# Windowed attention with sinks feeding a maxout FFN: another order for the opening and for chunk 3

## The chip, the cores and the metric

The kernel runs on one core of one Trainium2 chip. A core has five engines that run at the same time, each working through its own queue strictly in order: PE (TensorE, matrix products into PSUM), DVE (VectorE), ACT (ScalarE), POOL (GpSimd) and SP (SyncE, which here only issues transfers). PEld is the loading of weights into PE's array, which the profile lists apart from the products. Sixteen DMA engines, shared by all queues, move data between HBM (the main memory) and SBUF (the memory on the chip). PSUM, which takes PE's results, has 8 banks. The metric is the device time of one execution in microseconds (us), lower being better; a kernel's time is the median of its runs.

## The reference

The first half is attention over a window of 128 positions plus 4 sink positions, in 4 batches of 8 heads, 768 positions and 64 dimensions per head:

```python
scores = scale * np.matmul(q, k.transpose(0, 1, 3, 2))
keep = is_sink | in_window               # pos < 4, or 0 <= i - j < 128
scores = np.where(keep, scores, -1000000000.0)
a = np.exp(scores - max); a = a / (sum(a) + 1e-09)
attn = np.matmul(a, v)
```

The second half takes the heads side by side as `x` (3072 tokens of 512 numbers) through a feed-forward layer whose hidden part is the largest of three products:

```python
h = np.maximum(np.maximum(x @ w1, x @ w2), x @ w3)     # 3072 x 768
out = h @ w_out                                        # 3072 x 512
```

All inputs and the output are float32; the kernel computes in bfloat16 with float32 sums.

## The kernel before

The 3072 tokens are cut into 12 chunks of 256, three to a batch. `ci` is a chunk and `p` one of four pairs of heads; chunk 0 is the first of its batch and has no chunk ahead of it, so that its scores have three blocks (`lo = 1`), while chunk 1 has four and the sinks besides. The steps of a chunk are functions of the same name as here:

- `load` (L76) brings 512 KB of q, k or v in float32 into one of two buffers, on SP's queue. A `gate` is a tiny POOL instruction that writes into the buffer first, so that the transfer waits for POOL: `after(wi, c)` (L434) reads column c of weight `wi`, and so waits until the piece of the weight that holds this column has landed; `pool_gate` (L440) is a bare write.
- `cast_qk` and `cast_v` (L95, L104) turn this into bfloat16 on the engine named in the call. g = 0 stands for the pairs 0 and 1, g = 1 for the pairs 2 and 3.
- `turn` and `turn2` (L109, L129) are four PE transposes of q or k and a copy out of PSUM. From chunk 4 on `turn_dma` (L150) does this by a transposing transfer.
- `premask` (L251) lays the additive mask into the two PSUM banks of a pair of heads; `score` (L259) adds the products of q and k; `expo` (L282) takes the exponential on ACT and frees the banks. A pair without a `premask` is masked afterwards by a product on DVE, `mask` (L289).
- `sink_k`, `sink_score`, `sink_v` and `av_open` do the sinks. `av` (L339) multiplies by v, and divides on DVE (a reciprocal and a product) into `x_sb`.
- `xpose` (L364) is the turn of `x`: for each half t of the 256 tokens four PE transposes and one copy.
- `ffn_h(ci, fp, wi)` (L383) makes a third of the hidden layer for one of the three weights: 8 products over the columns 256 fp to 256 fp + 255 of weight `wi`, then a copy on ACT (`wi` = 0) or a maximum on DVE. `ffn_y` (L406) makes half of the output rows.
- `load_w` (L234) and `load_wo` bring the weights on POOL's queue. The transfer turns float32 into bfloat16, and its sizes are those of the bfloat16 side: 256 columns of a weight are 256 KB in the profile.
- `warm(n)` (L172) is n products of zeros, whose result is not used.

The order of the work is written out by hand. Each line of the list at L454-772 appends its instructions to the queues of the engines that it uses; nothing is reordered later. A queue waits at its first instruction whose inputs, or whose target (a buffer or a PSUM bank still being read), are not ready. PSUM banks are handed out in the order in which they were given back. The list is free until chunk 3; then `for i in range(3, NCH)` repeats a fixed interleaving in which chunk i's feed-forward part covers chunk i + 1's attention.

In what follows a third of a weight is named by its columns: w0[512:768] is the last third of the first of the three weights (`moe_w1` in the inputs), w1 is the second, w2 the third.

Of the kernel before, what the change touches and what calls it, by code (L numbers as in the profile page):

```python
# [9 lines left out]
F32 = mybir.dt.float32  # L10
# [6 lines left out]
def kernel(  # L17
# [13 lines left out]
    nc = tc.nc  # L31
# [3 lines left out]
    d_model = H * D  # L35
# [13 lines left out]
    with tc.manual_schedule():  # L49
# [122 lines left out]
        def warm(n):  # L172

            if n:
                pw = bank([128, 512], F32, "warm")
                for _ in range(n):
                    nc.tensor.matmul(pw, lhsT=wz[:, 0:128], rhs=wz, start=True, stop=True)  # L177
                give(pw)
# [160 lines left out]
        def av(ci, p):  # L339
            b, c = divmod(ci, CPB)  # L340
            o = os_[ci, p]
            e = es[ci, p][0]
            first = c == 0
            for t in range(2):
                for a in range(2):
                    blocks = [(1, ci, 0)] if t == 0 else [(2, ci, 0), (3, ci, 1)]
                    if t == 0 and c:
                        blocks = [(0, ci - 1, 1)] + blocks
                    for s, cv, n in blocks:
                        nc.tensor.matmul(  # L350
                            o[:, t, a], lhsT=e[:, a, s], rhs=vb[cv % RING][:, n, 2 * p + a],
                            start=first, stop=True, skip_group_check=True)
# [27 lines left out]

        hs = {}

        def ffn_h(ci, fp, wi, cuts=1):  # L383
            if ci not in hs:
                hs[ci] = work.tile([128, FB, 256], BF16, tag="h", bufs=3, name="h_sb")
            hp = bank([128, 2, 256], F32, "h_ps")
            for f in range(2):
                c0 = (2 * fp + f) * 128
                for ds in range(DS):
                    nc.tensor.matmul(  # L390
                        hp[:, f].rearrange("q (i t r) -> q i t r", i=2, t=2),
                        lhsT=w_sb[wi][:, ds, c0:c0 + 128],
                        rhs=xTs[ci][:, :, ds].rearrange("q t (i r) -> q i t r", i=2),
                        start=(ds == 0), stop=(ds == DS - 1))
            dst = hs[ci][:, 2 * fp:2 * fp + 2]
            if wi == 0:
                nc.scalar.copy(dst, hp)  # L397
            else:
                for f in range(cuts):
                    x = slice(2 * f // cuts, 2 * (f + 1) // cuts)  # L400
                    nc.vector.tensor_max(dst[:, x], dst[:, x], hp[:, x])  # L401
            give(hp)
# [2 lines left out]

        def ffn_y(ci, t, eng=None):  # L406
            if t == 0:
                ys[ci] = work.tile([128, 2, d_model], F32, tag="y", bufs=2, name="y_sb")
            yp = bank([128, d_model], F32, "y_ps")
            for fb in range(FB):  # L410
                nc.tensor.matmul(yp, lhsT=hs[ci][:, fb, t * 128:(t + 1) * 128], rhs=wo[:, fb],  # L411
                                 start=(fb == 0), stop=(fb == FB - 1))
            (nc.scalar.copy if eng is None else eng.tensor_copy)(ys[ci][:, t], yp)  # L413
            give(yp)

        def ffn_y_part(ci, t, c0, c1, eng):
            if t == 0 and c0 == 0:
                ys[ci] = work.tile([128, 2, d_model], F32, tag="y", bufs=2, name="y_sb")
# [36 lines left out]
        warm(5)  # L455
        load(0, 'k')
        load(0, 'q', part=0, parts=2)
        warm(2)
# [5 lines left out]
        warm(7)  # L464
        cast_qk(0, 'k', 0, nc.vector)
        cast_qk(0, 'k', 1, nc.gpsimd)
        cast_qk(0, 'q', 0, nc.gpsimd)
        premask(0, (0,))
        cast_qk(0, 'q', 1, nc.scalar)
        turn(0, 'k', 0, nc.vector)  # L470
        turn(0, 'k', 1, nc.scalar)
        turn(0, 'q', 1, nc.scalar)
        premask(0, (3,))
        load(1, 'k')
        turn(0, 'q', 0, nc.vector)
        score(0, (0,))
        premask(0, (2,))
        cast_v(0, 0, 0, nc.vector)
        cast_v(0, 1, 0, nc.gpsimd)
        cast_v(0, 1, 1, nc.vector)  # L480
        cast_qk(1, 'k', 0, nc.vector)
        premask(0, (1,))
        load(1, 'q')
        load_w(0, 512, 768)
        load_w(0, 0, 512)
        score(0, (1,))
        score(0, (2,))
        expo(0, 0)
        warm(3)
        sink_k(0)  # L490
        cast_v(0, 0, 1, nc.vector)
        expo(0, 1)
        load_w(1, 512, 768)
        turn2(1, 'k', 0, nc.vector)
        expo(0, 2)
        cast_qk(1, 'k', 1, nc.scalar)
        av_open(0)
        cast_qk(1, 'q', 0, nc.scalar)
        av(0, 0)
        score(0, (3,))  # L500
        sink_v(0)
        cast_qk(1, 'q', 1, nc.gpsimd)
        load_w(1, 0, 512)
        av(0, 1)
        load(1, 'v')
        expo(0, 3)
        turn(1, 'k', 1, nc.scalar)
        turn(1, 'q', 1, nc.vector)
        turn2(1, 'q', 0, nc.vector)
        cast_v(1, 0, 0, nc.gpsimd)  # L510
        cast_v(1, 1, 1, nc.gpsimd)
        cast_v(1, 1, 0, nc.gpsimd)
        cast_v(1, 0, 1, nc.gpsimd)
        premask(1, (0,))
        av(0, 3)
        load(2, 'k', part=0, parts=2, gate=after(0, 300))
        score(1, (0,))
        score(1, (2,))
        av(0, 2)
        load_w(2, 0, 256)  # L520
        load(2, 'k', part=1, parts=2)
        premask(1, (3,))
        score(1, (3,))
        expo(1, 0)
        xpose(0, 0, nc.vector)
        expo(1, 2)
        load(2, 'q', part=1, parts=2)
        load(2, 'q', part=0, parts=2, gate=pool_gate)
        xpose(0, 1, nc.vector)
        load_w(2, 256, 512)  # L530
        sink_score(1)
        load_w(2, 512, 768)
        premask(1, (1,))
        score(1, (1,))
        av_open(1)
        cast_qk(2, 'k', 1, nc.gpsimd)
        mask(1, 2)
        expo(1, 3)
        load(2, 'v', gate=after(0, 300))
        expo(1, 1)  # L540
        av(1, 0)
        load(3, 'q', gate=after(2))
        ffn_h(0, 2, 0)
        av(1, 2)
        av(1, 3)
        av(1, 1)
        cast_qk(2, 'k', 0, nc.scalar)
        load(3, 'k')
        ffn_h(0, 0, 0)
        ffn_h(0, 2, 1)  # L550
        ffn_h(0, 1, 0)
        xpose(1, 0, nc.vector)
        xpose(1, 1, nc.vector)
        ffn_h(0, 1, 1)
        ffn_h(1, 0, 0)
        ffn_h(0, 0, 1)
        load_wo()
        factors(msk0, addm0)
        ffn_h(1, 2, 0)
        turn(2, 'k', 0, nc.vector)  # L560
        ffn_h(1, 1, 0)
        ffn_h(1, 1, 1)
        turn(2, 'k', 1, nc.scalar)
        cast_v(2, 1, 0, nc.gpsimd)
# [64 lines left out]
        cast_v(3, 0, 0, nc.gpsimd)  # L629
# [12 lines left out]
        mask(3, 3)  # L642
# [173 lines left out]
```

## Time and profile before

| what | value |
|---|---|
| time, median of 3 runs | 178.46 us (178.2 to 179.15) |
| the profiled execution | 178.04 us, of which the span of the profile is 176.3 us |
| PE | 169.8 us busy, 96% of the span |
| PEld / DVE / ACT / POOL | 127.0 / 120.7 / 86.0 / 66.4 us busy |
| moved by DMA | 34.90 MB, 198 GB/s over the span |
| read from HBM / written | 25.17 MB / 6.29 MB |
| granted TensorE clock, mean | 0.997 |

The difference between 178.04 and 176.3 us lies ahead of the first and behind the last instruction of the profile. A busy PE is no sign that PE is at its best: the warm products count as busy, and the durations of pipelined products overlap. The distance between the starts of two products is what each of them takes of PE's time, and in the chain of work that ended last the pieces are given by that distance. The sixteen DMA engines together can show a busy share over 1, since packets overlap.

### The profile page before, as it was taken

What the parts mean: (1) busy time and instruction counts of PE and PEld (TensorE: products, weight loads), DVE (VectorE), ACT (ScalarE), POOL (GpSimd) and SP (SyncE); (2) the same over time, 40 slices, a digit from 0 to 9 for tenths busy, and PEclk for the clock granted to TensorE, in tenths of its full rate; (3) what the DMA queues carried; (4) which work ended last, traced back from release to release, by engine and by line L of the source; (5) the groups of instructions that cost most, each with busy time, mean ns of one, the idle gap of its engine ahead of it and who ended that gap; (6) DMA issues with size and microseconds to landing.
All of it is one profiled execution on the core that took longest, in us unless ns stands there. A gap on an engine that the chain in (4) does not pass through costs nothing.

```text
span 176.3 us, 4635 instructions
## 1 busy us (share of the span) xinstructions
PE 169.8 (96%) x1864; PEld 127.0 (72%) x1877; DVE 120.7 (68%) x262; ACT 86.0 (49%) x172; POOL 66.4 (38%) x126
## 2 busy tenths in 40 slices
PE   7889999999999999999999999999999999999992
PEld 2545999866786697697696796796795795796871
DVE  3387644796697895775775874875785775976451
ACT  4298455758844914914715814814617616420210
POOL 7596507623494693182172054245244000000000
PEclk9999999999999999999999999999999999999998
DMA  5999999999999999987999999999999218203203
GB/s 152 293 283 204 225 226 241 217 295 275 296 244 264 299 188 223 264 186 207 259 192 225 261 177 246 273 139 244 275 164 244 32 29 155 119 4 59 121 0 119
DMA packets 69637, 34.90 MB, mean 198 GB/s; under 512 B 26608, under 2 KB 68080, under 8 KB 69616
## 3 DMA queue, kind: packets, MB, share of 16 engines
q1 hardware_dynamic: 64976, 31.33, 81.1%
q0 software_dynamic: 4496, 3.15, 11.7%
q8 instruction: 14, 0.23, 0.5%
q10 hardware_dynamic: 144, 0.13, 0.2%
q14 instruction: 7, 0.06, 0.1%
HBM read 25.17 MB, written 6.29 MB: 178 GB/s over the span
## 4 chain that ended last, share of the span: by engine, by line
PE 88%; DMA 3%; POOL 3%; DVE 2%; issue 2%; POOLq 0%; SPq 0%; DVEq 0%
PE h_ps L390 52%; PE y_ps L411 17%; PE st L274 6%; PE o L350 6%; DMA v_raw<-in_v_dram 3%; PE pt L115 1%; PE xt L371 1%; DVE h_sb L401 1%; PE o L332 1%; PE sk L300 1%; PE st L256 1%; POOL w L237 1%; PE y_ps L421 1%; DVE e_sb L292 1%; POOL vb L105 0%
## 5 line engine op out<-in xcount | busy, mean ns | idle before, releaser
L390 PE MATMUL h_ps<-xT,w 128*128 128x256 bf16 x864 | 101.3, 273 | 0.1
L390 PEld LDWEIGHTS <-w 128*128 128x128 bf16 x864 | 82.0, 98 | 10.3 <-issue 0.4
L401 DVE TENSOR_TENSOR h_sb<-h_sb,h_ps 128x512 bf16<-128x512 bf16 (+1 forms) x74 | 49.1, 670 | 21.3 <-PE h_ps L390 18.1
L286 ACT ACTIVATE e_sb<-st 128x512 bf16<-128x512 f32 (+1 forms) x96 | 46.5, 577 | 8.0 <-PE st L274 8.0
L397 ACT CAST h_sb<-h_ps 128x512 bf16<-128x512 f32 x36 | 20.9, 585 | 46.9 <-PE h_ps L390 46.7
L105 POOL CAST vb<-v_raw 64x512 bf16<-64x512 f32 x44 | 29.6, 673 | 16.1 <-DMA v_raw<-in_v_dram 11.3
L411 PE MATMUL y_ps<-wo,h_sb 128*128 128x512 bf16 x126 | 31.9, 380 | 0.6
L292 DVE TENSOR_TENSOR e_sb<-e_sb,msk 128x1024 bf16<-128x1024 bf16 (+1 forms) x41 | 26.9, 694 | 0.9 <-ACT e_sb L286 0.8
L101 POOL CAST k_bf<-k_raw 128x512 bf16<-128x512 f32 x18 | 11.9, 679 | 40.5 <-DMA k_raw<-in_k_dram 28.5
L411 PEld LDWEIGHTS <-h_sb 128*128 128x128 bf16 x138 | 12.4, 98 | 14.4 <-issue 1.6
L358 DVE TENSOR_TENSOR x_sb<-o,rc 128x256 bf16<-128x256 f32 x48 | 20.4, 425 | 1.7
L413 DVE COPY y_sb<-y_ps 128x512 f32<-128x512 f32 x13 | 9.0, 692 | 14.2 <-PE y_ps L411 14.1
L350 PE MATMUL o<-vb,e_sb 128*128 128x65 bf16 x352 | 17.0, 194 | 0.3 <-DVE vb L105 0.3
L350 PEld LDWEIGHTS <-e_sb 128*128 128x128 bf16 x352 | 14.7, 97 | 3.0 <-issue 0.5
L274 PE MATMUL st<-qT,kT 64*128 64x128 bf16 (+1 forms) x256 | 14.4, 238 | 0.5 <-DVE qT L119 0.5
L274 PEld LDWEIGHTS <-kT 64*128 64x128 bf16 x256 | 8.4, 94 | 7.6 <-issue 5.7
L101 POOL CAST q_bf<-q_raw 128x512 bf16<-128x512 f32 x17 | 10.1, 618 | 6.9 <-DMA q_raw<-in_q_dram 6.8
L355 DVE RECIPROCAL rc<-o 128x4 f32<-128x4 f32 x48 | 8.5, 177 | 4.6 <-PE o L350 4.4
L306 ACT ACTIVATE e_sink<-sk 128x256 bf16<-128x256 f32 x8 | 3.1, 384 | 14.4 <-PE sk L300 14.4
L413 ACT COPY y_sb<-y_ps 128x512 f32<-128x512 f32 x10 | 5.8, 585 | 3.0 <-PE y_ps L411 2.7
L177 PE MATMUL warm<-wz 128*128 128x512 bf16 x16 | 5.6, 501 | 1.3 <-DVE wz L166 1.2
L237 POOL DMA_DIRECT2D w<-in_moe_w_dram x7 | 5.4, 773 | 0.0
(66 smaller groups left out, 68.8 us busy)
## 6 DMA issues: line engine op xcount, KB each, us to landing
k_raw<-in_k_dram SPq DMA_DIRECT2D x11, 512.0 KB, 5.1
v_raw<-in_v_dram SPq DMA_DIRECT2D x11, 512.0 KB, 7.4
out_dram<-y_sb SPq DMA_DIRECT2D x11, 512.0 KB, 3.2
q_raw<-in_q_dram SPq DMA_DIRECT2D x10, 512.0 KB, 7.3
w<-in_moe_w_dram POOLq DMA_DIRECT2D x5, 256.0 KB, 8.1
q_raw<-in_q_dram SPq DMA_DIRECT2D x4, 256.0 KB, 6.7
w<-in_moe_w_dram POOLq DMA_DIRECT2D x2, 512.0 KB, 8.9
wo<-in_moe_w_out_dram POOLq DMA_DIRECT2D x2, 384.0 KB, 8.1
```

Of the source, the lines that this page charges most:

```text
L101: f(x[:, 2 * g:2 * g + 2].rearrange("q p i a d -> q p a i d"), y[:, 4 * g:4 * g + 4].rearrange("q (p a) i d -> q p a i d", a=2))
L105: eng.tensor_copy(vb[ci % RING][64 * i:64 * i + 64, n, :, 0:D], raws[ci, "v"][64 * n:64 * n + 64, :, i])
L274: nc.tensor.matmul(st[a][:, s:s + q1 - q0].rearrange("q n (i r) -> q n i r", i=2), lhsT=x[hp, n, p].rearrange("q i r -> q (i r)"), rhs=qc[ ...
L286: nc.scalar.activation(e[:, a, lo:], st[a][:, lo:], AF.Exp, scale=scale)
L292: (eng or nc.vector).tensor_mul(e[:, :, lo:], e[:, :, lo:], msk0 if lo else msk)
L350: nc.tensor.matmul(o[:, t, a], lhsT=e[:, a, s], rhs=vb[cv % RING][:, n, 2 * p + a], start=first, stop=True, skip_group_check=True)
L358: nc.vector.tensor_mul(xs[ci][:, :, p], o[:, :, :, 0:D], rc.unsqueeze(3).to_broadcast([128, 2, 2, D]))
L390: nc.tensor.matmul(hp[:, f].rearrange("q (i t r) -> q i t r", i=2, t=2), lhsT=w_sb[wi][:, ds, c0:c0 + 128], rhs=xTs[ci][:, :, ds].rearrang ...
L397: nc.scalar.copy(dst, hp)
L401: nc.vector.tensor_max(dst[:, x], dst[:, x], hp[:, x])
L411: nc.tensor.matmul(yp, lhsT=hs[ci][:, fb, t * 128:(t + 1) * 128], rhs=wo[:, fb], start=(fb == 0), stop=(fb == FB - 1))
L413: (nc.scalar.copy if eng is None else eng.tensor_copy)(ys[ci][:, t], yp)
```

## The change

Three places of the order are changed, and four small things in the functions.

The opening (L454-561). Of chunk 0 the pairs 2 and 3 now come first: q's second half is cast and turned ahead of k, then k, then the scores of the pairs 2 and 3, then q's first half and the pairs 0 and 1. The list has 9 warm products in place of 17. All four `av` of chunk 0, and the first `xpose` of chunk 0, come ahead of the first scores of chunk 1. The pair 3 of chunk 1 has no `premask` any more and a `mask` on DVE instead. Of w0 and w1 every third is a transfer of its own, the last one first, in place of one transfer of 256 and one of 512 columns; between these issues on POOL's queue stand casts of chunk 1 (k first half, q first half, two of v) that had other places or engines, and `sink_k`. The three thirds of w2 are issued one behind the other after the gates of k and q of chunk 2. The first `ffn_h` of chunk 0 is copied by DVE and not by ACT.

The feed-forward part of chunks 0 and 1. The order was (chunk, third, weight) (0,2,0) (0,0,0) (0,2,1) (0,1,0), the turn of x of chunk 1, (0,1,1) (1,0,0) (0,0,1) (1,2,0) (1,1,0). It becomes (0,2,0) (0,1,0) (0,0,0) (0,2,1) (0,1,1), the turn of x of chunk 1, (0,0,1) (1,2,0) (1,1,0) (1,0,0). `load_wo` now stands ahead of the gate of q of chunk 3, and that gate reads column 300 of w2 instead of column 0, so it waits for w2[256:512].

Chunk 3 (L607-641). `ffn_y(1, 0)` comes ahead of the two turns of k of chunk 3, the turn of x of chunk 2 and `ffn_y(1, 1)` ahead of the scores of chunk 3; the casts of v of chunk 3 on POOL come together ahead of those of chunk 4; `store(0)` stands behind the two `turn_dma` of chunk 4.

The functions: `xs[ci]` is made by the first `av` of a chunk whichever pair that is, `ffn_h` can copy on another engine, and y has 4 buffers in place of 2.

```diff
             rc = work.tile([128, 2, 2], F32, tag="rc", bufs=4, name="rc")
-            if p == 0:
+            if ci not in xs:
...
-        def ffn_h(ci, fp, wi, cuts=1):
+        def ffn_h(ci, fp, wi, cuts=1, eng=nc.scalar):
...
-                nc.scalar.copy(dst, hp)
+                (nc.scalar.copy if eng is nc.scalar else eng.tensor_copy)(dst, hp)
...
-                ys[ci] = work.tile([128, 2, d_model], F32, tag="y", bufs=2, name="y_sb")
+                ys[ci] = work.tile([128, 2, d_model], F32, tag="y", bufs=4, name="y_sb")
```

The new opening as a whole (unchanged lines among them):

```python
load(0, 'q', part=1, parts=2)
warm(5)
load(0, 'k')
load(0, 'q', part=0, parts=2)
load(0, 'v', part=0, parts=2, gate=pool_gate)
load(0, 'v', part=1, parts=2)
masks()
sink_init()
factors(msk, addm)
cast_qk(0, 'q', 1, nc.scalar)
turn(0, 'q', 1, nc.scalar)
premask(0, (2,))
warm(4)
cast_qk(0, 'k', 1, nc.vector)
cast_qk(0, 'k', 0, nc.gpsimd)
cast_qk(0, 'q', 0, nc.gpsimd)
turn(0, 'k', 1, nc.vector)
load(1, 'k')
premask(0, (3,))
turn(0, 'k', 0, nc.scalar)
score(0, (2,))
score(0, (3,))
turn(0, 'q', 0, nc.vector)
premask(0, (0,))
load(1, 'q')
expo(0, 2)
cast_v(0, 1, 0, nc.gpsimd)
cast_v(0, 0, 0, nc.vector)
cast_v(0, 1, 1, nc.vector)
cast_v(0, 0, 1, nc.vector)
load_w(0, 512, 768)
load(1, 'v')
score(0, (0,))
expo(0, 3)
premask(0, (1,))
score(0, (1,))
expo(0, 0)
cast_qk(1, 'k', 0, nc.gpsimd)
load_w(0, 256, 512)
expo(0, 1)
av_open(0)
av(0, 2)
av(0, 3)
turn2(1, 'k', 0, nc.vector)
cast_qk(1, 'k', 1, nc.scalar)
av(0, 0)
cast_qk(1, 'q', 0, nc.gpsimd)
cast_qk(1, 'q', 1, nc.scalar)
turn(1, 'k', 1, nc.scalar)
av(0, 1)
premask(1, (0,))
premask(1, (1,))
turn2(1, 'q', 0, nc.vector)
turn(1, 'q', 1, nc.scalar)
xpose(0, 0, nc.vector)
sink_k(0)
cast_v(1, 0, 0, nc.vector)
cast_v(1, 1, 0, nc.vector)
load_w(0, 0, 256)
load_w(1, 512, 768)
score(1, (0,))
score(1, (1,))
expo(1, 0)
expo(1, 1)
xpose(0, 1, nc.vector)
cast_v(1, 1, 1, nc.gpsimd)
load_w(1, 256, 512)
cast_v(1, 0, 1, nc.gpsimd)
load_w(1, 0, 256)
sink_v(0)
sink_score(1)
score(1, (3,))
load(2, 'k', part=0, parts=2, gate=after(0, 300))
load(2, 'k', part=1, parts=2)
ffn_h(0, 2, 0, 1, nc.vector)
expo(1, 3)
score(1, (2,))
expo(1, 2)
load(2, 'q', part=1, parts=2)
load(2, 'q', part=0, parts=2, gate=pool_gate)
load_w(2, 0, 256)
load_w(2, 256, 512)
load_w(2, 512, 768)
mask(1, 3)
ffn_h(0, 1, 0)
mask(1, 2)
av_open(1)
cast_qk(2, 'k', 1, nc.gpsimd)
av(1, 0)
av(1, 1)
ffn_h(0, 0, 0)
load(2, 'v', gate=after(0, 300))
av(1, 3)
av(1, 2)
ffn_h(0, 2, 1)
ffn_h(0, 1, 1)
xpose(1, 0, nc.vector)
xpose(1, 1, nc.scalar)
ffn_h(0, 0, 1)
ffn_h(1, 2, 0)
cast_qk(2, 'k', 0, nc.scalar)
ffn_h(1, 1, 0)
ffn_h(1, 0, 0)
load_wo()
load(3, 'q', gate=after(2, 300))
load(3, 'k')
factors(msk0, addm0)
turn(2, 'k', 0, nc.vector)
ffn_h(1, 1, 1)
```

The part of it that was there before stood in this order from the first scores on:

```python
score(0, (0,))
premask(0, (2,))
cast_v(0, 0, 0, nc.vector)
cast_v(0, 1, 0, nc.gpsimd)
cast_v(0, 1, 1, nc.vector)
cast_qk(1, 'k', 0, nc.vector)
premask(0, (1,))
load(1, 'q')
load_w(0, 512, 768)
load_w(0, 0, 512)
score(0, (1,))
score(0, (2,))
expo(0, 0)
warm(3)
sink_k(0)
cast_v(0, 0, 1, nc.vector)
expo(0, 1)
load_w(1, 512, 768)
...
sink_v(0)
cast_qk(1, 'q', 1, nc.gpsimd)
load_w(1, 0, 512)
...
load(2, 'k', part=0, parts=2, gate=after(0, 300))
```

And chunk 3:

```diff
         turn(3, 'q', 1, nc.scalar)
-        turn(3, 'k', 1, nc.scalar)
         load(5, 'k', gate=after(0, 300))
         av(2, 1)
+        ffn_y(1, 0)
+        turn(3, 'k', 1, nc.scalar)
+        turn(3, 'k', 0, nc.scalar)
+        xpose(2, 0, nc.scalar)
+        xpose(2, 1, nc.vector)
+        ffn_y(1, 1)
         cast_qk(4, 'q', 1, nc.vector)
-        turn(3, 'k', 0, nc.scalar)
-        ffn_y(1, 0)
         cast_v(3, 1, 1, nc.gpsimd)
+        cast_v(3, 0, 0, nc.gpsimd)
+        cast_v(3, 0, 1, nc.gpsimd)
         score(3, (1,))
         cast_qk(4, 'q', 0, nc.vector)
         expo(3, 1)
         score(3, (0,))
-        xpose(2, 0, nc.scalar)
-        xpose(2, 1, nc.vector)
-        ffn_y(1, 1)
         cast_qk(4, 'k', 1, nc.gpsimd)
         mask(3, 1)
...
-        store(0)
         turn_dma(4, 'k')
         turn_dma(4, 'q')
+        store(0)
+        store(1)
         score(3, (2,))
-        store(1)
         expo(3, 0)
         expo(3, 3)
-        cast_v(3, 0, 1, nc.gpsimd)
```

More of the change, by code (lines that the diff above doesn't have):

```diff
@@ L479 @@
-        cast_v(0, 1, 0, nc.gpsimd)
-        cast_v(0, 1, 1, nc.vector)
-        cast_qk(1, 'k', 0, nc.vector)
+        cast_qk(0, 'q', 1, nc.scalar)
+        turn(0, 'q', 1, nc.scalar)
+        premask(0, (2,))
+        warm(4)
+        cast_qk(0, 'k', 1, nc.vector)
+        cast_qk(0, 'k', 0, nc.gpsimd)
+        cast_qk(0, 'q', 0, nc.gpsimd)
+        turn(0, 'k', 1, nc.vector)
+        load(1, 'k')
+        premask(0, (3,))
+        turn(0, 'k', 0, nc.scalar)
+        score(0, (2,))
+        score(0, (3,))
@@ L482 @@
+        turn(0, 'q', 0, nc.vector)
+        premask(0, (0,))
+        load(1, 'q')
+        expo(0, 2)
+        cast_v(0, 1, 0, nc.gpsimd)
+        cast_v(0, 0, 0, nc.vector)
+        cast_v(0, 1, 1, nc.vector)
+        cast_v(0, 0, 1, nc.vector)
+        load_w(0, 512, 768)
+        load(1, 'v')
+        score(0, (0,))
+        expo(0, 3)
         premask(0, (1,))
-        load(1, 'q')
-        load_w(0, 512, 768)
-        load_w(0, 0, 512)
         score(0, (1,))
-        score(0, (2,))
         expo(0, 0)
-        warm(3)
+        cast_qk(1, 'k', 0, nc.gpsimd)
@@ L490 @@
+        load_w(0, 256, 512)
+        expo(0, 1)
+        av_open(0)
+        av(0, 2)
+        av(0, 3)
+        turn2(1, 'k', 0, nc.vector)
+        cast_qk(1, 'k', 1, nc.scalar)
+        av(0, 0)
+        cast_qk(1, 'q', 0, nc.gpsimd)
+        cast_qk(1, 'q', 1, nc.scalar)
+        turn(1, 'k', 1, nc.scalar)
+        av(0, 1)
+        premask(1, (0,))
+        premask(1, (1,))
+        turn2(1, 'q', 0, nc.vector)
+        turn(1, 'q', 1, nc.scalar)
+        xpose(0, 0, nc.vector)
         sink_k(0)
-        cast_v(0, 0, 1, nc.vector)
@@ L508 @@
[L508 to L515, printed above, removed]
+        score(1, (0,))
+        score(1, (1,))
+        expo(1, 0)
+        expo(1, 1)
+        xpose(0, 1, nc.vector)
+        cast_v(1, 1, 1, nc.gpsimd)
+        load_w(1, 256, 512)
+        cast_v(1, 0, 1, nc.gpsimd)
+        load_w(1, 0, 256)
@@ L516 @@
+        sink_v(0)
+        sink_score(1)
+        score(1, (3,))
         load(2, 'k', part=0, parts=2, gate=after(0, 300))
-        score(1, (0,))
+        load(2, 'k', part=1, parts=2)
+        ffn_h(0, 2, 0, 1, nc.vector)
+        expo(1, 3)
         score(1, (2,))
[L519 to L525, printed above, removed]
         expo(1, 2)
@@ L528 @@
         load(2, 'q', part=0, parts=2, gate=pool_gate)
[L529 removed]
+        load_w(2, 0, 256)
         load_w(2, 256, 512)
[L531 removed]
         load_w(2, 512, 768)
[L533 to L534 removed]
+        mask(1, 3)
+        ffn_h(0, 1, 0)
+        mask(1, 2)
         av_open(1)
         cast_qk(2, 'k', 1, nc.gpsimd)
[L537 to L538 removed]
+        av(1, 0)
+        av(1, 1)
+        ffn_h(0, 0, 0)
         load(2, 'v', gate=after(0, 300))
[L540 to L543, printed above, removed]
+        av(1, 3)
         av(1, 2)
[L545 to L546 removed]
+        ffn_h(0, 2, 1)
+        ffn_h(0, 1, 1)
+        xpose(1, 0, nc.vector)
+        xpose(1, 1, nc.scalar)
+        ffn_h(0, 0, 1)
+        ffn_h(1, 2, 0)
         cast_qk(2, 'k', 0, nc.scalar)
+        ffn_h(1, 1, 0)
+        ffn_h(1, 0, 0)
+        load_wo()
+        load(3, 'q', gate=after(2, 300))
         load(3, 'k')
[L549 to L557, printed above, removed]
         factors(msk0, addm0)
[L559 removed]
         turn(2, 'k', 0, nc.vector)
[L561 removed]
         ffn_h(1, 1, 1)
```

30 lines of the change are left out of this document (1 added, 29 removed).

## The prediction

> **What bounds the kernel now.** I read the page first: PE is busy 96% of the span, so the question is where PE is not at useful work, and what feeds it there. From the page, the share of time that the sixteen DMA engines were busy, and their rate, in 40 slices of 4.41 us:
>
> ```profile
> DMA  5999999999999999987999999999999218203203
> GB/s 152 293 283 204 225 226 241 217 295 275 296 244 264 299 188 223 264 186 207 259 192 225 261 177 246 273 139 244 275 164 244 32 29 155 119 4 59 121 0 119
> ```
>
> DMA is full from the second slice on. Second, all that PE waited for, and the table of stages (us, busy us of PE, PEld, DVE, ACT, POOL, granted clock, DMA share, GB/s):
>
> ```profile
> PE warm L177 <- DVE wz L166: 1.2, 1, 1.2
> PE st L274 <- DVE qT L119: 0.5, 1, 0.5
> ...
> 8.00:13.00 5.00, 4.22 (x52) 2.19 (x53) 4.11 (x11) 4.14 (x11) 4.42 (x8) 1.00 1.22 288
> 13.00:18.00 5.00, 4.99 (x80) 3.05 (x79) 3.37 (x10) 4.22 (x10) 2.96 (x5) 1.00 1.34 203
> 22.00:32.00 10.00, 10.00 (x106) 9.09 (x104) 5.51 (x11) 5.47 (x10) 3.31 (x7) 1.00 1.22 230
> ```
>
> The waits lie before 12 us, and from 13 us on PE is never idle to speak of. The time is therefore the opening plus a sum of PE work which the change hardly touches. An opening that gets PE ready earlier pays only if what PE then needs is there. Third, the chain that ended last (start, us, what) at the end of the opening:
>
> ```profile
> 18.01 0.87 PE h_ps L390 x8
> 18.88 0.72 PE o L350 x24
> ...
> 22.67 3.49 PE h_ps L390 x32
> ...
> 26.17 0.22 PE pt L115 x4
> 26.39 1.75 PE h_ps L390 x16
> ```
>
> One `ffn_h` costs 0.87, one turn 0.22. I mark a point that both orders share: the turn of k's first half of chunk 2 and the nine steps (0,2,0) (0,1,0) (0,0,0) (0,2,1) (0,1,1) (0,0,1) (1,2,0) (1,1,0) (1,0,0) are done. Before, that is after the first eight products of the last row: 26.39 + 0.87 = 27.26. Behind it both lists are alike until chunk 3, so the shift of this point is the shift of all that follows.
>
> **The change, part by part: the weights.** Nine `ffn_h` need w0 and w1, so I follow POOL's queue, which issues them (timeline, POOL and then SP), and the landings (us from issue to landing, from the DMA view of the stretch around each issue):
>
> ```profile
> 8.45 0.84 POOL L105 CAST vb<-v_raw 64x512 bf16<-64x512 f32 x1 [1.30 <-DMA v_raw<-in_v_dram]
> 9.23 1.71 POOL L237 DMA_DIRECT2D w<-in_moe_w_dram  x2
> 10.99 0.50 POOL L228 COPY ks<-kT 64x16 bf16<-64x16 bf16 x2
> 12.22 0.61 POOL L101 CAST q_bf<-q_raw 128x512 bf16<-128x512 f32 x1
> 12.77 0.74 POOL L237 DMA_DIRECT2D w<-in_moe_w_dram  x1
> 13.76 2.58 POOL L105 CAST vb<-v_raw 64x512 bf16<-64x512 f32 x4 [0.25 <-DMA v_raw<-in_v_dram]
> 18.68 0.18 POOL L437 CAST k_raw<-w 1x1 f32<-1x1 bf16 x1 [2.34 <-DMA w<-in_moe_w_dram]
> 18.80 0.74 POOL L237 DMA_DIRECT2D w<-in_moe_w_dram  x1
> 19.57 1.48 POOL L237 DMA_DIRECT2D w<-in_moe_w_dram  x2
> ```
>
> ```profile
> 3.83 0.72 SPq L90 DMA_DIRECT2D k_raw<-in_k_dram  x1
> 4.60 1.71 SPq L90 DMA_DIRECT2D q_raw<-in_q_dram  x1
> 6.35 1.71 SPq L90 DMA_DIRECT2D v_raw<-in_v_dram  x1
> 18.88 0.92 SPq L90 DMA_DIRECT2D k_raw<-in_k_dram  x2
> ```
>
> ```profile
> k_raw<-in_k_dram SPq DMA_DIRECT2D x1, 512.0 KB, 6.2
> q_raw<-in_q_dram SPq DMA_DIRECT2D x1, 512.0 KB, 7.3
> v_raw<-in_v_dram SPq DMA_DIRECT2D x1, 512.0 KB, 7.4
> w<-in_moe_w_dram POOLq DMA_DIRECT2D x1, 256.0 KB, 5.5
> w<-in_moe_w_dram POOLq DMA_DIRECT2D x1, 512.0 KB, 9.4
> w<-in_moe_w_dram POOLq DMA_DIRECT2D x1, 256.0 KB, 5.8
> w<-in_moe_w_dram POOLq DMA_DIRECT2D x1, 256.0 KB, 9.8
> ```
>
> Of chunk 1, k lands at 3.83 + 6.2 = 10.0, q at 4.60 + 7.3 = 11.9, v at 6.35 + 7.4 = 13.75; SP's order is unchanged, so these stay. The weights' rows belong to the issues at 9.23 (w0[512:768], landed 14.7), 12.77 (w1[0:512], landed 22.2), 18.80 (w2[0:256], landed 24.6) and 20.31 (w2[512:768], landed 30.1). Before, the last of w1 landed at 22.2, and PE came to it at 22.67 with no wait: the weights were just in time already.
>
> POOL after: alike to 10.2, where the first issue ends. Then the cast of k (0.61) to 10.8; w0[256:512] (0.74) to 11.55; the cast of q waits for 11.9, to 12.5; `sink_k` (0.50) to 13.0; w0[0:256] to 13.75; w1[512:768] to 14.5; a cast of v (2.58 / 4 = 0.64) to 15.1; w1[256:512] to 15.9; a cast to 16.5; **w1[0:256] only now, at 16.5 to 17.25**, where the same columns were issued at 12.77 before. The gate of chunk 2's k is next, 17.4; it waits for w0[256:512] alone and not for all of w0, so this load starts at 17.4 where it was 18.88.
>
> Landings after. Alone, 256 KB take 0.262 MB / 203 GB/s = 1.29. w0[256:512]: 14.7 + 1.3 = 16.0. w0[0:256]: 17.3 if the stream has no gap; 18.5 by the shortest row (5.5 behind its issue at 13.0). I take 18.3, nearer to the row, since only 1.3 of its 5.5 us is moving and the rest stays whatever the stream does. w1[512:768]: 19.6. From about 19 the loads of chunk 2, k and with the gates gone also q, run beside it. The price beside loads is w2[0:256] behind w1: 24.6 - 22.2 = 2.4; the next two took 30.1 - 24.6 = 5.5, 2.75 each. I take 2.45: w1[256:512] 22.05, **w1[0:256] 24.5**. Its ends: 16.5 + 5.5 = 22.0 and 16.5 + 9.8 = 26.3.
>
> The Trainium skill (DMA: Bandwidth & Descriptors, section SWDGE vs HWDGE vs iDMA) says that each DMA engine takes turns between the internal queues of software-issued and other transfers. By that a third would wait for as many loaded bytes, 1.29 + 0.262 MB / 288 GB/s = 2.2, an estimate; w1[0:256] would land at 24.0 and the sum below be 0.5 lower. The trace has 2.4 to 2.75, so it agrees in kind and is dearer.
>
> **PE behind them.** In the new order (0,0,1), which reads w1[0:256], stands ahead of (1,2,0) (1,1,0) (1,0,0), which need w0 alone: 2.6 us of ready work queue behind the wait. So the marked point comes at 24.6 + 4 x 0.87 + 0.22 = 28.3, against 27.26: **+1.04**. What comes ahead is hidden by this wait: the eight warm products fewer (PE waited there anyway), the pairs' order, the turn of x ahead of chunk 1's scores, one `premask` fewer, `ffn_h` copied by DVE. Without that cover they gain: the copy of chunk 0's second x waits on DVE behind two casts of v (13.75 + 2 x 0.64 = 15.0), so the first `ffn_h` starts at 15.5 instead of 18.01. From there to the marked point before took 9.25; after adds 22 small products (one `av`, `av_open`, `score(1, 2)`; 0.03 each by the chain's 24 in 0.72, the scores' more), 0.8 in all: 25.55.
>
> The longer gate of chunk 3's q (now w2[256:512], which I put at 24.5 + 2 x 2.7 = 29.9): behind it wait on POOL `factors` and the casts of chunk 2's v, on SP q and k of chunk 3.
>
> ```profile
> 38.57 0.72 POOL L101 CAST q_bf<-q_raw 128x512 bf16<-128x512 f32 x1 [3.21 <-DMA q_raw<-in_q_dram]
> 40.38 0.22 PE pt L115 x4
> ```
>
> q landed at 38.5 and its turn came at 40.38: 1.1 us of slack behind the cast, and PE is a us later. DMA is full meanwhile, so a later issue takes a later place, not more time: 0, up to 1 if q came two us late. The stores behind `turn_dma`, with 4 buffers of y: nothing reads them, 0.
>
> **Chunk 3.** PE is not idle here, so nothing is to be won; but DVE has little room (DVE's timeline, PE's, then the chain):
>
> ```profile
> 48.00 0.69 DVE L401 TENSOR_TENSOR h_sb<-h_sb,h_ps 128x512 bf16<-128x512 bf16 x1 [1.32 <-PE h_ps L390]
> 48.60 1.87 DVE L292 TENSOR_TENSOR e_sb<-e_sb,msk 128x768 bf16<-128x768 bf16 x2
> ...
> 49.65 0.54 PE L350 MATMUL o<-vb,e_sb 128*128 128x65 bf16 x12
> ...
> 43.75 0.55 PE xt L371 x8
> 44.31 1.29 PE y_ps L411 x6
> ```
>
> `score(3, 1)` moves behind the turn of x and the `ffn_y` of the last two rows, 1.84 us, and with it on DVE its mask and, queued behind that, a cast of k and one of v. DVE's 1.32 us of idle time takes up most; 0.5 is left, by which the masks come late that `av(3, 0)` waits for on PE. **+0.5**, from 0 (if ACT, which comes between, catches up) to 0.8. The casts of v that POOL does earlier hide behind these masks.
>
> Sum: 178.04 (the profiled execution: 176.3 of span and 1.74 around it) + 1.04 + 0.5 = 179.6. That execution lies 0.42 under the median of 178.46, so I forecast **180.0**, 0.9% slower. About 0.5%, 0.9 us, is what a measurement of this kernel can tell from no change.
>
> **Rivals.** *The weights are not late* (faster): POOL's issues run ahead, or loads take less of the stream, and PE runs its list through: 25.55 at the marked point, -1.7, + 0.5: 177.3. For it: PE starts the FFN 2.5 us earlier, and issues in thirds give w0[256:512] at 16.0 instead of 18.7. Against: it needs w1[0:256] by 21.9, 5.4 behind its issue, where the shortest row has 5.5. It decides at 23.0 (23.1 + 3.7 + 0.5 = 27.3), 6.5 behind the issue: earlier gains, later loses. *A draw*: landing between 22.1 and 23.9, the sum within 0.9 us: 178.5. *The change loses more*: w1[0:256] takes the 9.8 of w2[512:768], lands at 26.3: 30.1 at the mark, +2.8, + 0.8: 182.1.
>
> *A cold PE.* 14 warm products of 512 columns take
>
> ```profile
> 1.20 4.83 PE L177 MATMUL warm<-wz 128*128 128x512 bf16 x14 [1.20 <-DVE wz L166]
> ```
>
> 0.345 each, where products of 256 columns take 3.49 / 32 = 0.109 later: the first were at half speed. Five, a pause, and four may leave PE slow until 8 us: 4 x 0.22 us more in the warm ones and a little on turns, 1.1 in all on chunk 0. Ahead of late weights it costs nothing (PE has 24.6 - 21.9 = 2.7 to spare); in the first rival it takes the gain down to 178.4. The Trainium skill (TensorE: Matmul & The Clock Gate, section Part 1: The HAM clock gate) has PE at half rate until about 3.4 us of sustained activity; by it 8 or 9 of the 14 were slow, and the trace's 0.345 agrees. It speaks against this change, not for it.
>
> **Chances.** Late weights as forecast 0.55, 179.0 to 181.3 (landing 23.9 to 25.7); the worse case 0.08; the draw 0.13; weights in time 0.24, of which a fifth is lost to the cold PE and so no change. A tenth of the forecast falls under 0.9 us if chunk 3 costs nothing. Slower by over 0.5%: 0.55 x 0.9 + 0.08 = 0.57; within 0.5%: 0.06 + 0.13 + 0.05 = 0.24; faster 0.19. The range for 8 in 10 is 177.9 to 181.4: one in ten is left out on each side.
>
> **What would show it.** Right: PE waits of 1 us and more for w (or `h_ps` waiting on DMA) between 19 and 25 us; the last issue of w1 at 16.5 on POOL; the marked point near 28.3. Wrong: no such wait and the point under 27; then the gain stays to the end. For chunk 3: `av(3, 0)` waiting for DVE's mask. The prediction fails if the 2.45 beside loads is wrong by more than 0.7, or if POOL's casts don't hold up the issues.

## The result, and the profile after

The changed kernel takes 179.37 us (median; 178.36 to 181.21), the kernel before, in the same comparison, 178.20 us (177.85 to 179.15): a ratio of 1.0061, with a 95% interval of 1.0047 to 1.0076. That is 1.2 us slower by the medians, 1.1 by the ratio. One execution of the changed kernel, the one of 181.21 us, was in a slower state and is left out of the ratio; the highest of the others is 180.65. The profiled execution of the changed kernel has a span of 177.8 us against 176.3 us, 1.5 us more.

From the page, DMA's busy share and rate; what PE waited for; and stages (columns as in the prediction):

```profile
DMA  5999999999999999996997999998999405203203
GB/s 155 294 280 194 207 219 219 219 299 284 285 147 287 306 198 213 267 264 169 237 247 189 250 205 229 262 174 223 269 171 250 39 17 165 118 4 59 118 2 118
```

```profile
PE warm L177 <- DVE wz L166: 1.2, 1, 1.2
PE pt L115 <- ACT q_bf L101: 1.0, 1, 1.0
PE o L350 <- DVE vb L105: 0.8, 1, 0.8
PE sk L300 <- DMA qT<-q_bf: 0.6, 1, 0.6
PE h_ps L390 <- ACT e_sb L286: 0.5, 1, 0.5
```

```profile
8.00:13.00 5.00, 4.03 (x46) 2.32 (x45) 2.65 (x6) 4.01 (x11) 3.68 (x7) 1.00 1.22 287
13.00:18.00 5.00, 4.28 (x71) 2.79 (x69) 4.72 (x15) 3.58 (x8) 4.91 (x10) 1.00 1.45 194
18.00:28.40 10.40, 10.40 (x132) 8.80 (x132) 6.43 (x15) 5.98 (x13) 2.88 (x6) 1.00 1.33 212
```

No wait for a weight is among them. PE waits before its first feed-forward step, is then busy without a gap until 28.4 us, and waits once more, 0.6 us, much later: before the sinks of chunk 5, for a transposed q. The chain has both places:

```profile
17.92 1.03 PE h_ps L390 x8
...
24.63 3.54 PE h_ps L390 x32
28.16 0.22 PE pt L115 x4
...
65.81 4.55 DMA qT<-q_bf
70.36 0.04 issue
70.41 0.29 PE sk L300 x4
```

The marked point lies at 28.16 + 0.22 = 28.38, against 27.26: +1.12. The first of the 32 products is the step (0,0,1), which needs w1[0:256]. That third was issued when the forecast said, but landed at 16.48 + 6.4 = 22.9, 1.6 us earlier than forecast, and 1.7 us ahead of its use (POOL's timeline, then the landings of the third and of the first load of chunk 2's k, issued at 17.51):

```profile
16.48 0.74 POOL L237 DMA_DIRECT2D w<-in_moe_w_dram  x1
```

```profile
w<-in_moe_w_dram POOLq DMA_DIRECT2D x1, 256.0 KB, 6.4
k_raw<-in_k_dram SPq DMA_DIRECT2D x1, 256.0 KB, 7.1
```

So PE itself was late. It was not late against the kernel before, whose first feed-forward step stands at 18.01 in the chain (17.92 here), but against the 15.5 that the forecast gave it. From that step to the marked point PE now needs 10.46 us (17.92 to 28.38), where the kernel before needed 9.25: the new order has more of chunk 1's attention behind that step, 0.8 us by the forecast's own count, and the earlier start that was to pay for it did not come. PE's timeline at the start, and DVE's:

```profile
1.20 2.31 PE L177 MATMUL warm<-wz 128*128 128x512 bf16 x5 [1.20 <-DVE wz L166]
4.50 0.61 PE L115 MATMUL pt<-ident,q_bf 128*128 128x128 bf16 x4 [0.99 <-ACT q_bf L101]
...
5.54 1.91 PE L177 MATMUL warm<-wz 128*128 128x512 bf16 x4
7.25 0.63 PE L115 MATMUL pt<-ident,k_bf 128*128 128x128 bf16 x4
```

```profile
10.48 1.82 DVE L105 CAST vb<-v_raw 64x512 bf16<-64x512 f32 x3
...
31.63 0.43 DVE L101 CAST q_bf<-q_raw 128x512 bf16<-128x512 f32 x1 [0.48 <-DMA q_raw<-in_q_dram]
```

The five warm products end at 3.5 us, PE pauses for 1.0, and the next four take 1.7 us from start to start of what follows, 0.43 each, where a product of that size takes 0.22 later in the kernel: half speed. The granted clock reads 1.00 in all these stretches, so that the half speed is read from the starts alone. The first turn of k stands behind them and starts at 7.25 instead of 6.19. All of chunk 0 follows from it, the casts of v too, which wait on DVE's queue behind a copy of turned q though v landed at 8.5. The last row is of another kind: q of chunk 2 landed only at 31.6 (30.5 before), just ahead of its turn at 32.16. DMA is a us behind as well, and in this execution it does not show as a wait of PE, because PE is as late.

### The profile page after: what moved, and what is told of

The parts are those of the page before. It is cut to its first block, busy times and chain, and to the rows that moved or that the text cites. A ratio compares the mean times of both kernels' runs of the same rounds, so it can differ in the third digit from the quotient of the medians.

```text
span 177.8 us, 4618 instructions
## 1 busy us (share of the span) xinstructions
PE 169.2 (95%) x1855; PEld 126.5 (71%) x1867; DVE 121.2 (68%) x263; ACT 86.6 (49%) x173; POOL 66.7 (37%) x127
## 4 chain that ended last, share of the span: by engine, by line
PE 78%; DMA 9%; DVE 3%; POOL 3%; ACT 2%; issue 2%; SPq 1%
PE h_ps L390 44%; PE y_ps L411 16%; DMA q_raw<-in_q_dram 7%; PE st L274 6%; PE o L350 5%; DMA qT<-q_bf 3%; PE pt L115 2%; DVE vb L105 1%; ACT e_sb L286 1%; POOL vb L105 1%; PE warm L177 1%; POOL q_bf L101 1%; PE o L332 1%; SPq L90 1%; PE y_ps L421 1%
## 5 line engine op out<-in xcount | busy, mean ns | idle before, releaser
L105 POOL CAST vb<-v_raw 64x512 bf16<-64x512 f32 x42 | 27.0, 643 | 20.1 <-DMA v_raw<-in_v_dram 17.2
L237 POOL DMA_DIRECT2D w<-in_moe_w_dram x9 | 6.9, 771 | 0.0
L177 PE MATMUL warm<-wz 128*128 128x512 bf16 x9 | 4.2, 630 | 1.2 <-DVE wz L166 1.2
```

Of the source, the lines that this page charges most:

```text
L105: eng.tensor_copy(vb[ci % RING][64 * i:64 * i + 64, n, :, 0:D], raws[ci, "v"][64 * n:64 * n + 64, :, i])
```

## The experiments

The starts of five steps in each profiled execution (us), the span, and the ratio to the kernel before with its 95% interval. A profile is of one execution; the ratios are of many.

| kernel | first turn of k | first FFN step | first scores, chunk 2 | sinks, chunk 4 | sinks, chunk 5 | span | ratio |
|---|---|---|---|---|---|---|---|
| before | 6.19 | 17.85 | 32.23 | 55.15 | 68.87 | 176.3 | 1 |
| changed | 7.25 | 17.92 | 33.35 | 56.03 | 70.41 | 177.8 | 1.0061 (1.0047 to 1.0076) |
| changed, old chunk 3 | 7.18 | 17.67 | 33.11 | 56.17 | 69.89 | 177.3 | 1.0035 (1.0012 to 1.0058) |
| before, new chunk 3 | 6.95 | 18.22 | 32.60 | 55.40 | 69.26 | 176.7 | 0.9987 (0.9967 to 1.0006) |
| changed, 8 warm products | 6.65 | 16.19 | 33.48 | 56.24 | 70.29 | 177.7 | 1.0029 (1.0006 to 1.0053) |
| changed, no second warm group | 6.15 | 16.20 | 32.60 | 55.16 | 68.88 | 176.3 | 1.0033 (1.0003 to 1.0063) |
| before, w0 and w1 in thirds | 7.13 | 18.57 | 32.96 | 56.09 | 69.81 | 177.2 | 1.0051 (1.0027 to 1.0075) |
| 8 warm, wide weights | 6.64 | 16.29 | 32.80 | 55.47 | 69.51 | 176.9 | 1.0066 (1.0037 to 1.0096) |
| 8 warm, (0,0,1) later | 6.27 | 16.07 | 33.30 | 56.09 | 70.09 | 177.5 | 1.0031 (1.0009 to 1.0053) |
| 8 warm, old chunk 3 | 6.18 | 15.97 | 33.05 | 56.30 | 70.02 | 177.4 | 1.0046 (1.0027 to 1.0064) |
| before, no w2 | 6.59 | 18.38 | 32.76 | 55.36 | 69.08 | 176.6 | 0.9978 (0.9961 to 0.9994) |
| changed, no w2 | 7.28 | 17.69 | 33.12 | 55.61 | 69.82 | 177.2 | 0.9993 (0.9967 to 1.0019) |
| 8 warm, no w2 | 6.37 | 16.04 | 32.13 | 54.62 | 68.71 | 176.1 | 0.9992 (0.9968 to 1.0016) |
| 8 warm, wide pairs, stores first | 6.74 | 16.41 | 33.03 | 57.84 | 71.56 | 179.0 | 1.0102 (1.0060 to 1.0145) |

Three openings ran in two kernels each, which differ only from chunk 3 on. At the first scores of chunk 2 the two executions lie 0.37 us apart for the old opening (32.23 and 32.60), 0.24 for the new one (33.35 and 33.11) and 0.43 with 8 warm products (33.48 and 33.05). So a difference of 0.4 us between two rows of the table tells nothing, and the profiled execution of the kernel before is an early one: its first turn of k is at 6.19, at 6.59 to 7.13 in the three other kernels that start like it. The +1.12 at the marked point overstates the difference by some tenths.

**PE's own lateness: more warm products, or fewer.** The first edit closes the pause, the second takes away what stands in front of the turn of k.

```diff
-        warm(5)
+        warm(8)
```

> The changed kernel with 8 warm products at the start in place of 5, so that PE is busy from 1.2 us until the first turn at 4.5 without a pause. If late weights hold PE up (the forecast): no change, 179.4. If the pause keeps PE at half speed until about 9 us (the rival called a cold PE): the four warm products behind the first turn take 0.9 in place of 1.7, the first turn of k starts at 6.1 to 6.3 and not at 7.25, the first feed-forward step at 16.9 and not 17.9; the time falls by 0.5 to 1.0, less than by 1.0 if PE then waits longer for the transposed q of chunk 5. The spread between runs, wider than that of the kernel before, shrinks as well by this theory.

```diff
-        warm(4)
```

> The changed kernel without the four warm products ahead of the first turn of k. Late weights (the forecast): no change, 179.4. Cold PE: the four products themselves (1.7 us at half speed) are no longer in the way of the turn of k, which starts at 6.0 to 6.3, but PE stays at half speed for longer, so that turns and scores of chunk 0 take double until 9 us or later; the first feed-forward step comes at 17.0 to 17.9, the time falls by 0 to 0.8. If only the place of the four products counts and not the clock, this gains as much as eight warm products at the start.

With 8 products the first feed-forward step comes 1.7 us earlier. PE's timeline, then DVE's:

```profile
1.20 3.60 PE L177 MATMUL warm<-wz 128*128 128x512 bf16 x8 [1.20 <-DVE wz L166]
...
5.65 1.16 PE L177 MATMUL warm<-wz 128*128 128x512 bf16 x4
6.65 0.39 PE L115 MATMUL pt<-ident,k_bf 128*128 128x128 bf16 x4
...
16.19 1.03 PE L390 MATMUL h_ps<-xT,w 128*128 128x256 bf16 x8 [0.47 <-ACT e_sb L286]
...
23.84 3.67 PE L390 MATMUL h_ps<-xT,w 128*128 128x256 bf16 x32 [0.94 <-DMA w<-in_moe_w_dram]
...
33.48 0.84 PE L274 MATMUL st<-qT,kT 64*128 64x128 bf16 x18
```

```profile
31.79 0.43 DVE L101 CAST q_bf<-q_raw 128x512 bf16<-128x512 f32 x1 [1.28 <-DMA q_raw<-in_q_dram]
```

The first turn of k takes 0.39 or 0.40 us in all six profiled executions with 8 warm products, and 0.61 to 0.63 in all four with the pause: the pause did keep PE slow. But the gain is gone by the first scores of chunk 2: now (0,0,1) waits 0.94 us for w1[0:256], the wait of the forecast, and then the cast of chunk 2's q, for which DVE sat idle 1.28 us, is late, so the scores come at 33.48 instead of 33.35. The ratio falls by 0.0032, or 0.6 us, uncertain by 0.003; that is the low end of what the theory of a cold PE expected, and half of the loss is left.

PE's timeline without the second group:

```profile
6.15 0.61 PE L115 MATMUL pt<-ident,k_bf 128*128 128x128 bf16 x4 [0.37 <-DVE k_bf L101]
...
16.20 1.03 PE L390 MATMUL h_ps<-xT,w 128*128 128x256 bf16 x8 [0.39 <-DVE xT L372]
```

The turn of k starts earlier still, at half speed, the first feed-forward step is as early as with 8 products, and the ratio is as good, 1.0033. By what was expected of this run, that speaks for the place of the four products and not for PE's speed; but PE is at full speed sooner here too (a turn at 8.19 takes 0.40 us, one at 8.32 in the changed kernel 0.63), so that the two are not told apart. Its profiled execution ends at 176.3; the median, 179.17, says that most executions do not. What is left of the loss fits two limits of about the same size, one behind the other: PE's late start, and the transfers.

**Is it the order behind the wait?**

```diff
-        ffn_h(0, 0, 1)
         ffn_h(1, 2, 0)
...
         ffn_h(1, 0, 0)
+        ffn_h(0, 0, 1)
```

> The changed kernel with 8 warm products, and the step (0,0,1), which reads the last third of w1, moved behind (1,2,0) (1,1,0) (1,0,0), which need w0 alone. If the 0.94 us wait for w with ready work queued behind it is the loss, PE has no wait for w, the end of this group comes 0.9 earlier, and the time falls by up to 0.9 to 178.0. If DMA as a whole is the limit, PE then waits for q of chunk 2 (which it already did for 0.4 to 0.8 with 8 warm products) and the time falls by less than 0.3.

PE's timeline, then DVE's:

```profile
23.51 3.67 PE L390 MATMUL h_ps<-xT,w 128*128 128x256 bf16 x32 [0.74 <-DVE xT L372]
...
32.09 0.40 PE L115 MATMUL pt<-ident,q_bf 128*128 128x128 bf16 x4 [0.55 <-DVE q_bf L101]
...
31.61 0.43 DVE L101 CAST q_bf<-q_raw 128x512 bf16<-128x512 f32 x1 [1.44 <-DMA q_raw<-in_q_dram]
```

PE has no wait for w left. But (1,2,0), which now comes first, needs the turn of x of chunk 1, and PE waits 0.74 us for DVE's copy of it, so that of the 0.94 only 0.2 is gone: the edit does not free the ready work, and its price, the 2.6 us of the forecast, is not tested by it. What the run does show is the next limit: the cast of q waits for DMA even longer (1.44 us), PE waits 0.55 for that cast, and the scores of chunk 2 come at 33.30. 1.0031 is no different from 1.0029.

**DMA's part.** The third weight is not brought (its products read w1), which takes load off the DMA queues between 18 and 30 us (DMA's share falls from 1.28 to 1.02 there in the changed kernel):

```diff
+            if wi == 2:
+                return
```

> The kernel before without the transfers of the third weight; its products read w1 in its place, so all products stay, and some 4 us of DMA time are left out between 18 and 30 us. The control: PE has no wait for DMA in the kernel before, so the time stays at 178.2 to 178.4.

> The changed kernel without the transfers of the third weight, whose products read w1. If the full DMA queues alone make the change slower, the loss is gone: 178.0 to 178.4. If PE at half speed sets its opening by itself (the marked point at 28.4 with or without w2), the loss stays but for the wait for the transposed q of chunk 5: 178.9 to 179.3.

> The changed kernel with 8 warm products and without the transfers of the third weight, whose products read w1. If there are two limits of about the same size, the cold PE and behind it the DMA queues, taking both away gives what neither gave alone: the first feed-forward step at 16.2, the marked point at 26.6 to 27.0, the time 177.3 to 177.9, under the kernel before. If there is a third limit, 178.3 or more.

PE's timelines of the second and of the third (helpers have moved by three lines, L277 is the scores):

```profile
33.12 0.84 PE L277 MATMUL st<-qT,kT 64*128 64x128 bf16 x18
```

```profile
23.27 3.67 PE L393 MATMUL h_ps<-xT,w 128*128 128x256 bf16 x32 [0.52 <-DMA w<-in_moe_w_dram]
...
32.13 0.84 PE L277 MATMUL st<-qT,kT 64*128 64x128 bf16 x18
```

At the first scores of chunk 2 a late PE with freed queues gives 33.12; 8 warm products with full queues 33.48, and 33.05 in the other kernel with that opening; both limits 33.35, and 33.11; neither 32.13. Taking away one limit changes no more than executions differ anyway; taking away both gives about a us. This rests on one or two executions of each case, and the one without the second warm group, its queues as full, was at 32.60. In the times, the control gains 0.0022, the changed kernel 0.0068; so 0.0046 of its 0.0061 goes with the DMA load, uncertain by 0.003, and what is left against the control, 0.0015, is within that uncertainty. The medians are less kind: 178.73, between the two forecasts for this run, against 178.20 for the control. With both limits away I expected less than the kernel before has, or 178.3 and more if there is a third limit. The profiled execution is at the first (176.1); the median, 178.41, and the ratio, 0.9992, are at the second. What the 8 warm products add once the queues are free is not shown by the times, and a third limit is not excluded.

**Thirds, and wide pieces.** In the kernel before, the two wide transfers are split in two:

```diff
-        load_w(0, 0, 512)
+        load_w(0, 256, 512)
+        load_w(0, 0, 256)
...
-        load_w(1, 0, 512)
+        load_w(1, 256, 512)
+        load_w(1, 0, 256)
```

> The kernel before with w0[0:512] and w1[0:512] each brought as two transfers of 256 columns, issued one behind the other at the old places. If smaller pieces cost DMA time (a piece of 256 columns arrives in packets half as long), the last third of w1 lands 0.5 to 1.0 later than 22.2, and PE, which used it at 22.7 to 24, waits 0 to 0.5: 178.4 to 178.9. If only the places of the issues matter: 178.4, and the first third of the pair lands earlier.

```profile
1.20 5.77 PE L177 MATMUL warm<-wz 128*128 128x512 bf16 x14 [1.20 <-DVE wz L166]
```

It is 0.5% slower: 179.05, more than the 178.9 that was the dearer end. The cause is not settled. In the profiled execution PE nowhere waits for w, and its lateness is there at the first turn of k, where the program is still that of before; the same 14 warm products took 5.77 us and not 4.83. From that turn to the first scores of chunk 2 it needs 25.8 us, no more than the 26.0 of the kernel before. What does differ is POOL's DMA queue (packets, MB, share of 16 engines' span), before and in thirds:

```profile
q0 software_dynamic: 4496, 3.15, 11.7%
q0 software_dynamic: 5552, 3.15, 12.5%
```

The changed kernel has the second row too. Whether these 1056 packets more are what costs the 0.5% is not shown; if they are, they are most of what the change loses. The reverse, wide pieces in the changed kernel with 8 warm products:

```diff
-        load_w(0, 256, 512)
+        load_w(0, 0, 512)
...
-        load_w(0, 0, 256)
...
-        load_w(1, 256, 512)
+        load_w(1, 0, 512)
...
-        load_w(1, 0, 256)
```

> The changed kernel with 8 warm products, and w0 and w1 in pieces of 256 and 512 columns as before, each wide piece issued where its first third was. Late weights as the limit behind the cold PE: w1[0:512] is issued at about 14.5 in place of 15.1 and 16.5, lands by 22, the wait of 0.94 us for w that showed with 8 warm products is gone; the time falls from 178.9 to 178.0 to 178.4, if the loads of chunk 2 do not hold PE up instead by as much. If the weights are no limit: 178.9. What the wide piece costs is w0[256:512], which lands with w0[0:256], at about 17.6, a few tenths behind its first use at 17.5.

The wait for w was to go and the time to fall to 178.0 to 178.4. The scores of chunk 2 come earlier in the profile (32.80 for 33.48 and 33.05), but PE still waits 0.8 us for w, in two places, and 1.0066 is no gain: a miss.

**Chunk 3.** Its old order in the changed kernel, its new order in the kernel before, and its old order with 8 warm products:

> The changed kernel with the old order of chunk 3. Theory of the forecast (late weights, and a DVE that makes chunk 3 dearer by 0.5): the marked point stays at 28.3 to 28.4, the time falls by 0.5 to about 178.9. Rival (the new chunk 3 saves 0.2 on PE at first, but holds up SP's queue by 2 us, so that the transposed q of chunk 5 lands late and PE waits 0.6 for it): this wait goes and the 0.2 saved goes with it, 178.9 to 179.1. Told apart in the trace: by the first theory PE waits at the av of chunk 3 in the changed kernel; by the second it waits before the sink scores of chunk 5, and here no longer.

> The kernel before with the new order of chunk 3 (and 4 buffers of y) and the old opening. Theory of the forecast: slower by 0.5, 178.7, by a wait of the av of chunk 3 for DVE's masks. Rival (SP's queue held up): slower by 0.4 or more, because PE comes to chunk 5 earlier by a us than in the changed kernel and the transposed q no earlier; the wait before the sink scores of chunk 5 is 0.6 to 1.5 us. If the new chunk 3 is harmless alone: 178.2.

> The changed kernel with 8 warm products and the old order of chunk 3. If the clock's part (0.5 us between the two kernels) and chunk 3's (0.4) add, 178.5; the wait for the transposed q of chunk 5 (0.3 with 8 warm products) is 0. If the wait moves with PE's earlier arrival, nothing is gained by the old order: 178.9.

The edit is the chunk 3 part of the diff, turned round or alone. Alone it does nothing that can be measured (0.9987). In the changed kernel the old order takes off 0.0026, uncertain by 0.003, and the wait before chunk 5's sinks, 0.6 us, is gone. With 8 warm products it takes off nothing (1.0046 against 1.0029). From chunk 2's scores to chunk 4's sinks PE needs 22.68 us in the changed kernel and 23.06 with the old order: the new order saves 0.4 there (0.1 with the old opening, 0.5 with 8 warm products), and no wait of PE for a mask is in the profile. From there to chunk 5's sinks it gives back 0.7 (0.1 and 0.3), so that in sum it lies within 0.3 us of nothing in all three pairs. What it costs lies on SP. SP's timeline of the changed kernel, then of the kernel before:

```profile
53.26 1.02 SPq L427 DMA_DIRECT2D out_dram<-y_sb  x2
...
61.38 4.34 SPq L159 DMA_TRANSPOSE kT<-k_bf  x2
65.81 1.27 SPq L154 DMA_TRANSPOSE qT<-q_bf  x1
```

```profile
58.38 5.28 SPq L159 DMA_TRANSPOSE kT<-k_bf  x2
63.76 1.26 SPq L154 DMA_TRANSPOSE qT<-q_bf  x1
```

SP comes to the transposes of chunk 5 3.0 us later than before, 2.0 of it by the order of chunk 3, since with the old order in the changed kernel it comes to them at 59.38; how much of the 2.0 the stores make is not separated. The transposed q, 4.55 us on its way, lands at 70.4, where PE has been waiting since 69.8. In the kernel before it landed at 63.76 + 5.0 = 68.8, a tenth ahead of its use. With the new chunk 3 alone SP is 1.9 us later than before as well (60.30), but PE does not wait.

**A try at a faster kernel.** 8 warm products, (0,0,1) later, weights in wide pairs, and the stores ahead of the transposes of chunk 4:

```diff
+        store(0)
+        store(1)
         turn_dma(4, 'k')
         turn_dma(4, 'q')
-        store(0)
-        store(1)
```

> A try at a faster kernel, nothing left out: the changed kernel with 8 warm products, (0,0,1) behind the steps that need w0 alone, the weights in wide pieces where they are needed late (w0 and w1 as 512 and then 256 columns, w2 as 512 and 256), and both stores ahead of the transposes of chunk 4 instead of behind them. If the halved packets were what kept the DMA queues half a us behind, the first half of q of chunk 2 lands by 30.6 to 31.0 and the wait for the transposed q of chunk 5 goes: 178.0 to 178.5, a draw with the kernel before or a little under it. If the queues are full anyway: 178.7 to 179.0 as with 8 warm products.

The profile of it, what PE waited for, and SP's timeline:

```profile
PE sk L300 <- DMA qT<-q_bf: 1.6, 1, 1.6
```

```profile
46.85 2.94 SPq L427 DMA_DIRECT2D out_dram<-y_sb  x2
49.90 3.28 SPq L159 DMA_TRANSPOSE kT<-k_bf  x2
```

1% slower, the slowest of all, and beyond both forecasts for it: the two stores hold SP for 2.94 us, the transposes of chunk 4 start 1.3 us later than in the changed kernel, and PE waits 1.6 us for them before chunk 4's sinks. No version beat the kernel before beyond its interval, apart from the control that leaves a transfer out.

## Why the prediction was right, and where it was not

**The number and the sign.** 1.5 us slower was forecast, 1.2 measured, well inside the range, and the marked point came at 28.38 for a forecast of 28.3. The cause it gave is not the one that this execution shows: of its own signs, there is no wait for w, and yet the point is not under 27.

**The step that failed: w1[0:256] landing at 24.5.** It landed at 22.9. The price of 2.45 for a third beside loads was laid on both last thirds of w1, because the loads of chunk 2 started at 17.4. They did (17.51), but the first of them landed 7.1 us later and not the 4.1 of the kernel before. w1[512:768] landed at 19.35 for a forecast of 19.6, the other two thirds at 21.2 and 22.9: 1.9 and 1.6 apart, the last 0.8 under the price, more than the 0.7 that the prediction allowed itself. In the five other profiled executions with this opening and all three weights in thirds the same two landed at 20.9 to 21.3 and at 23.0 to 23.8. So the first was earlier than its forecast of 22.05 every time, and the price for the second, 1.9 to 2.9, held in some executions and not in this one. The Trainium skill (DMA: Bandwidth & Descriptors, section SWDGE vs HWDGE vs iDMA) has a DMA engine take turns between its queues; that agrees with the 2.4 to 2.75 of the kernel before, not with the 1.9 and 1.6 of this execution, which are less than the 2.2 that the forecast estimated by it.

**What stood in its place.** The first feed-forward step was put at 15.5 and came at 17.92, so that the 0.8 us of work moved behind it was not covered. The rival of a cold PE had this: four warm products at 0.43, the turn of k at 7.25, about 1.1 late. Its sentence that this costs nothing ahead of late weights failed because the weights were not late here. With 8 warm products the step came at 16.0 to 16.4 in six profiled executions, so the 15.5 itself was too early by more than half a us; in the first of them the late weight and behind it the late q showed at once, 0.94 us and 1.28 us of idle time. So the mechanism of the forecast is real and second in line; both limits end at 33.1 to 33.5. That the number came out right, because the two limits are of about the same size, is luck: the forecast did not name the one that acts first.

**Hidden items.** That the fewer warm products cost nothing was wrong: with three of them back the first feed-forward step came 1.7 us earlier and the ratio fell by 0.0032. The longer gate of chunk 3's q at no cost held: its turn came at 41.34 without a wait. So did the earlier casts of v.

**Chunk 3, +0.5 by DVE's masks.** Wrong in mechanism: PE did not wait for a mask and the stage got 0.4 shorter. The queue that should have been followed is SP's: 0 was written for the stores behind the transposes, because nothing reads them; what stands behind them on SP is the next chunks' loads, and a wait of 0.6 us for chunk 5's q came of it all. The old order takes 0.0026 off the ratio, uncertain by 0.003; that this is the 0.5 us of the forecast is luck.

**What stays open.** How the loss divides between PE's late start and DMA in a typical execution: the profiles show one each, the lead of either varies by up to a us between executions, and the ratios do not add up (8 warm products gain 0.003 with full queues and nothing with free ones). Whether thirds in themselves cost anything: in the kernel before they cost 0.5%, nearly the whole loss, and no row says where. Neither was tried further.

## What to carry to other kernels

Where the DMA queues are full and PE hardly waits, as here over the first three quarters of the time, an opening can be bound twice: before moving work ahead, list the landing of every transfer against its use, as slack, and expect a gain no larger than the smallest slack that follows. Fillers that bring PE to full speed are part of the schedule: a pause of a us among them, and three fillers fewer, went here with a first feed-forward step 1.7 us later. A step that nothing reads is not free if it stands in a queue that feeds others.

## What the runs showed of the hardware

The same 14 warm products, with nothing ahead of them, took 4.83 us in one execution and 5.77 in another, as PE came to full speed sooner or later; this moves the first turn of k by 0.9 us in kernels that are alike up to there. The granted clock reads 1.00 in the profile's rows throughout. The changed kernel, which comes to full speed later still, spreads over 2.3 us (178.36 to 180.65) where the kernel before spreads over 1.3; that the one is the cause of the other is not shown. The Trainium skill (TensorE: Matmul & The Clock Gate, section Part 1: The HAM clock gate) says that the point where PE changes to full rate varies from run to run; the traces agree, with 0.9 us. A load issued on SP while converting transfers of POOL are under way landed 7.1 us after its issue, against 4.1 for the same load issued 1.4 us later in the kernel before, where such transfers were under way too; why is not shown.
